# Attention with two kinds of heads, then a maxout network: another order for the first half batch and for each later step

## Chip, cores and metric

The kernel runs on one core of one Trainium2 chip. The metric is the device time of one execution in microseconds (us); before the change the median of three runs is 235.67 us (235.42 to 236.05).

## What is computed

Four batches of eight heads of causal attention over 768 positions with 64 numbers per head. Heads 0, 2 and 6 see every earlier position, the others only the first 4 positions and a window of the last 64. Each row of the result (8 heads x 64 = 512 numbers) then goes through a network that takes the largest of three products and multiplies that by a fourth matrix.

```python
scores = scale * np.matmul(q, k.transpose(0, 1, 3, 2))
stream_keep = causal & (is_sink | in_win)
mask = np.where(retr[0, :, 0, 0, None, None], full_mask, stream_mask)
scores = np.where(mask[None, :, :, :], scores, -1000000000.0)
...
return np.matmul(a, v).astype(np.float32)

h = np.maximum(np.maximum(x @ w1, x @ w2), x @ w3)
return (h @ w_out).astype(np.float32)
```

Here `x` is the attention's result as 3072 rows of 512, `w1` to `w3` are 512 x 768 and `w_out` is 768 x 512.

## The kernel before

**Steps.** The work is cut into 32 attention steps, numbered s. A step is one pair of heads in one half of one batch's rows (384 rows, three blocks of 128): steps 0 to 3 are the four head pairs of the first half of batch 0, steps 4 to 7 those of its second half, steps 8 to 11 the first half of batch 1, and so on. In a first half a step has two units of scores (0 and 1), in a second half, where a row also looks back at the first half, four (0 to 3). The score tiles `st` have two buffers in PSUM, so a unit of scores can only start when the exponential of the unit two before it has read its buffer. Transposes (`tr`), attention sums (`oacc`) and the network's results (`yy`) share four other PSUM buffers in turn.

**Stages of a step.** `load(s)` (L113) issues the DMAs of q and k for one pair of heads (192 KB each), and, once for each half batch, three DMAs of 256 KB for v of all eight heads. `prep(s)` (L283) casts k to fp16 on DVE (`kn`) and q on ACT (`qn`). `turn(s)` (L310) transposes both on PE, six matmuls, and copies the result to `KQ` on DVE. `scores(s, units)` (L329) does the score matmuls on PE, takes their exponential on ACT (into `pt`), and multiplies the blocks that need it by a 0/1 mask `mk`: on POOL, but for unit 1 of steps 0 to 3, which DVE does. `prep_v(s)` (L291) casts v (`va`; on ACT in steps 0 to 3, later on DVE) and makes on POOL a copy `vf` whose far blocks are zero for the windowed heads. `av(s)` (L380) multiplies `pt` by `va` or `vf` on PE; its seventh matmul is the first that reads `vf`. DVE then takes a reciprocal (`rc`) and a product (`x`). `turn_x(s)` (L407) transposes `x` on PE, and DVE copies it to `xT`.

**The network.** When the fourth head pair of a half batch is turned, `ffn` (L219) for its 384 rows is put into a queue of 24 units. A unit of the first 18 is four matmuls into one `yy` tile (L238) and its evacuation: ACT copies the product with the first matrix (L246), DVE takes the maximum with the other two (L249). The last six are three groups of six matmuls with `w_out` (L256), each followed by an ACT copy and an output DMA, and by an empty unit. For the first half batch the 18 units go matrix by matrix, so that the first six need only `w1`. `share(s, part, 3)` (L427) hands out these units at three places of each step, from step 5 on, 24 for each four steps.

**What sets the order.** Nothing reorders the program: each engine does its instructions in the order in which the loop at L447 writes them, and waits where an operand isn't ready. A step writes: the load for step s+7, `scores(s)` of units 0 and 1, `turn_x(s-2)`, a share, `turn(s+1)`, `av(s-1)`, a share, `prep(s+2)`, `scores(s)` of units 2 and 3, `prep_v(s+1)`, a share. In steps 1 to 4 `turn_x(s-1)` follows right behind `av(s-1)`. The masks of the head pairs 2 and 3 are built by `head_masks` (L195, four DVE instructions) in steps 1 and 2, and each of steps 0 to 3 ends with `load_weight` (L205), a DMA issued by POOL of one weight matrix (768 KB in fp16). All other loads and the outputs are issued by SP, but for q of steps 0 to 3 (ACT).

Of the kernel before, what the change touches and what calls it, by code (L numbers as in the profile page):

```python
# [10 lines left out]
FP32 = mybir.dt.float32  # L11
AF = mybir.ActivationFunctionType
ALU = mybir.AluOpType
# [35 lines left out]
def kernel(  # L49
# [32 lines left out]
    AHEAD = 7  # L82

    consts = ctx.enter_context(tc.tile_pool(name="consts", bufs=1))
    stage = ctx.enter_context(tc.tile_pool(name="stage", bufs=AHEAD + 1))
# [23 lines left out]

# [3 lines left out]
    def load(s):  # L113
        b, half, hp = where(s)
        hs, ts = slice(2 * hp, 2 * hp + 2), slice(half * HALF, (half + 1) * HALF)
        t = []
        for nm, src in (("ks", k), ("qs", q)):
            st = stage.tile([P, 2, HB, D], FP32, tag=nm, name=nm)
            eng = nc.scalar if s < NHP and nm == "qs" else nc.sync
            eng.dma_start(  # L120
                out=st, in_=src[b, hs, ts].rearrange("h (p j) d -> p h j d", p=P)
            )
            t.append(st)
        staged[s] = t
        if hp == 1:
            vs = stage.tile([P, H, HB, D], FP32, tag="vs", name="vs", bufs=3)
            for j in range(HB):
                r0 = half * HALF + j * P
                nc.sync.dma_start(
                    out=vs[:, :, j], in_=v[b, :, r0 : r0 + P].rearrange("h p d -> p h d")  # L130
                )
            staged_v[b, half] = vs
# [150 lines left out]
    def prep(s):  # L283
# [3 lines left out]
        nc.vector.tensor_copy(out=kn, in_=ks_.rearrange("p h j d -> p j h d"))  # L287
# [41 lines left out]
    def scores(s, us):  # L329
# [21 lines left out]
        for u, st in zip(us, sts):  # L351
# [4 lines left out]
            for at, u0, nu, cols, n, m0 in MASKED[half]:  # L356
                if at != u:
                    continue
                for hl_all in (slice(0, 2),):
                    if nu == 1 and len(cols) == 1:  # L360
                        x = pt[:, u0, hl_all, cols[0] : cols[0] + n]
                        m = mk[:, 2 * hp : 2 * hp + 2, m0 : m0 + n]
                    elif nu == 2:
                        x = pt[:, u0 : u0 + 2, :, cols[0] : cols[0] + n]
                        m = (
                            mk[:, 2 * hp : 2 * hp + 2, m0 : m0 + n]
                            .unsqueeze(1).to_broadcast([P, 2, 2, n])
                        )
                    else:
                        x = pt[:, u0].rearrange("p h (c n) -> p h c n", n=n)[:, :, 0:4:3]  # L370
                        m = (
                            mk[:, 2 * hp : 2 * hp + 2, m0 : m0 + n]
                            .unsqueeze(2).to_broadcast([P, 2, 2, n])
                        )
                    eng = nc.vector if s < NHP and u == 1 else nc.gpsimd
                    eng.tensor_tensor(out=x, in0=x, in1=m, op=ALU.mult)  # L376
# [30 lines left out]
    def turn_x(s):  # L407
        b, half, hp = where(s)
# [17 lines left out]

    def share(s, part, parts):  # L427
        if s < FIRST or s > NSTEP:
            return
# [16 lines left out]
    prep_v(0)  # L446
    for s in range(NSTEP + 2):  # L447
# [6 lines left out]
        if s > FIRST:  # L454
            turn_x(s - 2)
        share(s, 0, 3)
        if s + 1 < NSTEP:
            turn(s + 1)
        if 0 < s <= NSTEP:
            av(s - 1)  # L460
        if 0 < s < FIRST:
            turn_x(s - 1)
        share(s, 1, 3)
        if s + 2 < NSTEP:
            prep(s + 2)
        if live and n_u > 2:
            scores(s, [2, 3])
        if s + 1 < NSTEP:
            prep_v(s + 1)
        if 0 < s < NHP - 1:  # L470
            head_masks(s + 1)
        share(s, 2, 3)
        if s < 4:
            load_weight(s)
# [37 lines left out]
```

## Time and profile before

| | before |
|---|---|
| median of three runs | 235.67 us |
| the profiled execution | 235.46 us |
| its span, first to last instruction | 233.7 us |
| PE busy | 203.3 us (87%) |
| DVE, ACT, POOL busy | 144.2, 131.2, 121.0 us |

The profiled execution is 1.76 us longer than its span, which lies around the instructions. The profile has a page (busy time of each engine, the span in 40 slices, the chain of work that ended last, the costliest groups of instructions by line) and the trace answers for any stretch: busy time by window, what each engine waited for, and the instructions in order of time. A row of the order of time reads: start, duration, engine, line, operation, output<-inputs, form, count, and in square brackets how long the engine had been idle and on whom it waited. Neighbouring instructions of one kind are merged into one row. An engine name with q behind it (POOLq, SPq) or a DMA row is an issue, not the transfer.

### The profile page before, as it was taken

Reading aid. Unit: us, or ns where it says so; the run is one execution under the profiler, and the core shown is the slowest. Engines: PE = TensorE matmul, PEld = TensorE weight load, DVE = VectorE, ACT = ScalarE, POOL = GpSimd, SP = SyncE. Lnnn points to the kernel's source line nnn. Section 1 sums busy time; section 2 is a strip of 40 time slices with the busy share of each in tenths; the row PEclk is TensorE's granted clock in tenths of the full one; section 3 lists DMA queues with packets and bytes.
Section 4 is the critical chain, followed back from the end, with each engine's and each line's share of the span. In section 5 each row is a group of like instructions: output and inputs, shape, how many; then the busy total and the mean of one; then the engine's idle time right before and its main releaser. Section 6 shows DMA issues by size and latency. Waiting matters only on the chain.

```text
span 233.7 us, 5102 instructions
## 1 busy us (share of the span) xinstructions
PE 203.3 (87%) x2000; PEld 120.8 (52%) x2000; DVE 144.2 (62%) x306; ACT 131.2 (56%) x206; POOL 121.0 (52%) x137
## 2 busy tenths in 40 slices
PE   1335458999999999999999999999999999999993
PEld 0123333566556645655566545665566556555651
DVE  2437771488778854657689817766689636552540
ACT  3065347664675556785664586556655568742222
POOL 3066657256775717754777444577766276550000
PEclk9999999999999999999999999999999999999998
DMA  5999999980369226900497039402300120003003
GB/s 127 272 271 230 245 235 216 319 181 6 107 195 228 81 78 174 222 3 4 157 270 181 3 135 237 104 0 66 139 3 1 48 90 3 0 0 137 1 0 135
DMA packets 48359, 28.64 MB, mean 123 GB/s; under 512 B 26576, under 2 KB 45264, under 8 KB 48336
## 3 DMA queue, kind: packets, MB, share of 16 engines
q1 hardware_dynamic: 44736, 24.39, 39.3%
q0 software_dynamic: 2368, 3.15, 7.6%
q10 hardware_dynamic: 1232, 0.79, 1.2%
q8 instruction: 15, 0.25, 0.5%
q14 instruction: 8, 0.07, 0.1%
HBM read 25.17 MB, written 6.29 MB: 135 GB/s over the span
## 4 chain that ended last, share of the span: by engine, by line
PE 68%; ACT 11%; POOL 3%; issue 3%; DVE 2%; POOLq 0%; ACTq 0%; DVEq 0%
PE yy L238 34%; ACT pt L353 9%; PE oacc L391 8%; PE yy L256 8%; PE st L343 6%; PE tr L315 4%; POOL pt L376 3%; PE tr L416 3%; PE yst L238 3%; ACT qn L288 1%; PE yst L256 1%; DVE KQ L322 1%; DVE x L401 0%; POOLq L507 0%; DVE pt L376 0%
## 5 line engine op out<-in xcount | busy, mean ns | idle before, releaser
L376 POOL TENSOR_TENSOR pt<-pt,mk 128x512 f16<-128x512 f16 (+1 forms) x92 | 97.3, 1078 | 64.4 <-ACT pt L353 64.2
L353 ACT ACTIVATE pt<-st 128x1024 f16<-128x1024 f32 x96 | 82.5, 922 | 20.0 <-PE st L343 13.4
L246 ACT CAST acc<-yy 128x384 f16<-128x384 f32 x45 | 21.8, 488 | 44.4 <-PE yy L238 39.6
L343 PE MATMUL st<-KQ 64*128 64x384 f16 (+2 forms) x320 | 31.2, 297 | 11.3 <-DVE KQ L322 7.3
L238 PE MATMUL yy<-xT,w0t 128*128 128x384 f16 x180 | 38.1, 335 | 0.0
L249 DVE TENSOR_TENSOR acc<-yy,acc 128x384 f16<-128x384 f32 x45 | 24.8, 554 | 20.4 <-ACT acc L246 11.8
L322 DVE COPY KQ<-tr 128x768 f16<-128x768 f16 x32 | 30.4, 951 | 10.6 <-PE tr L315 10.6
L238 PE MATMUL yy<-xT,w1t 128*128 128x384 f16 x180 | 36.2, 326 | 0.0
L238 PE MATMUL yy<-xT,w2t 128*128 128x384 f16 x180 | 36.1, 326 | 0.0
L302 POOL TENSOR_TENSOR vf<-va,far 128x130 f16<-128x130 f16 (+1 forms) x32 | 20.0, 625 | 23.9 <-DVE va L300 14.2
L256 PE MATMUL yy<-woutt,hT 128*128 128x512 f16 x132 | 31.0, 379 | 0.0
L419 DVE COPY xT<-tr 128x384 f16<-128x384 f16 x32 | 11.4, 356 | 30.4 <-PE tr L416 30.4
L343 PEld LDWEIGHTS <-KQ 64*128 64x128 f16 x320 | 13.1, 98 | 32.5 <-issue 20.3
L391 PE MATMUL oacc<-va,pt 128*128 128x65 f16 x352 | 27.1, 199 | 0.8 <-POOL pt L376 0.4
L249 DVE TENSOR_TENSOR hT<-yy,acc 128x384 f16<-128x384 f32 x45 | 25.0, 555 | 3.3 <-PE yy L238 0.3
L391 PEld LDWEIGHTS <-pt 128*128 128x128 f16 x672 | 25.5, 100 | 1.6 <-POOL pt L376 1.2
L263 ACT COPY ot<-yy 128x512 f32<-128x512 f32 x22 | 12.9, 588 | 19.5 <-PE yy L256 19.5
L238 PEld LDWEIGHTS <-w0t 128*128 128x128 f16 x192 | 18.0, 100 | 10.9 <-issue 1.6
L238 PEld LDWEIGHTS <-w2t 128*128 128x128 f16 x192 | 17.8, 98 | 11.2 <-issue 0.8
L238 PEld LDWEIGHTS <-w1t 128*128 128x128 f16 x192 | 17.3, 97 | 11.8 <-issue 2.4
L391 PE MATMUL oacc<-vf,pt 128*128 128x65 f16 x320 | 22.1, 194 | 0.0
L256 PEld LDWEIGHTS <-hT 128*128 128x128 f16 x144 | 13.3, 98 | 14.6 <-issue 0.6
(46 smaller groups left out, 159.8 us busy)
## 6 DMA issues: line engine op xcount, KB each, us to landing
ks<-in_k_dram SPq DMA_DIRECT2D x32, 192.0 KB, 4.1
vs<-in_v_dram SPq DMA_DIRECT2D x24, 256.0 KB, 5.8
out_dram<-ot SPq DMA_DIRECT2D x24, 256.0 KB, 2.0
qs<-in_q_dram SPq DMA_DIRECT2D x28, 192.0 KB, 4.0
qs<-in_q_dram ACTq DMA_DIRECT2D x4, 192.0 KB, 6.2
w0t<-in_moe_w_dram POOLq DMA_DIRECT2D x1, 768.0 KB, 8.5
w1t<-in_moe_w_dram POOLq DMA_DIRECT2D x1, 768.0 KB, 10.0
w2t<-in_moe_w_dram POOLq DMA_DIRECT2D x1, 768.0 KB, 11.0
```

Source lines behind the costliest of these rows:

```text
L238: nc.tensor.matmul(yy[:, 0:HALF], w_t[wi][:, ks, ni * P : (ni + 1) * P], xT[b, half][ks], start=(ks == 0), stop=(ks == KS - 1),)
L246: nc.scalar.copy(out=acc[ni], in_=yy[:, 0:HALF])
L249: nc.vector.tensor_tensor(out=dst, in0=yy[:, 0:HALF], in1=acc[ni], op=ALU.max)
L256: nc.tensor.matmul(yo[:, 0:DMdl], hT[ns][:, tb * P : (tb + 1) * P], woutt[:, ns, :], start=(ns == 0), stop=(ns == NNB - 1),)
L263: nc.scalar.copy(out=ot, in_=yo[:, 0:DMdl])
L302: nc.gpsimd.tensor_tensor(out=vf[j][:, hs, k0:k1, 0 : D + 1], in0=va[j][:, hs, k0:k1, 0 : D + 1], in1=far[:, hs, k0:k1].unsqueeze(3).to_br ...
L322: nc.vector.tensor_copy(out=KQs[s].rearrange("p (i t j) -> p i t j", i=2, j=HB), in_=tr[:, 0:S].rearrange("p (i j t) -> p i t j", i=2, j=HB),)
L343: nc.tensor.matmul(st[:, hl, c0 : c0 + n * P], KT[ki // HB if half else 0][hb : hb + D, ki % HB * P : (ki % HB + 1) * P], KQ[hb : hb + D, ...
L353: nc.scalar.activation(out=pt[:, u, :, 0:w], in_=st[:, :, 0:w], func=AF.Exp, scale=sc)
L376: eng.tensor_tensor(out=x, in0=x, in1=m, op=ALU.mult)
L391: nc.tensor.matmul(o[:, qi, hl, 0 : D + 1], pt[:, u, hl, c : c + P], vv[:, 2 * hp + hl, ki, 0 : D + 1], start=(idx == 0), stop=(idx == len ...
L419: nc.vector.tensor_copy(out=xT[b, half][hp], in_=tr[:, 0:HALF])
```

## The change

It does five things.

1. **Loads.** q and k come for two pairs of heads at once (384 KB) from step 2 on, into tiles for four heads, six buffers of each; loads are issued eight steps ahead instead of seven; v is loaded behind q and k of the steps 2 and 3 in the first half batch, and at the first head pair of each later half batch.
2. **The first four steps** have a loop of their own. In it the masks are no longer part of `scores`: those on DVE stand behind `turn(s+1)` and `av(s-1)`. `turn_x` comes two steps late there too. `prep_v` of steps 0 and 1 stands behind the scores of step 1. `kn` of the steps 2, 3 and 4 is cast on ACT. The four mask-building instructions for the head pairs 2 and 3 stand together at the end of step 1.
3. **The weights** are issued in steps 1, 2, 4 and 4 instead of 0, 1, 2 and 3.
4. **The first network** starts in step 4 instead of step 5, because `turn_x` of steps 2 and 3 both stand there; a table `EARLY` hands out its 24 units as 7, 6, 4, 3 and 4 in steps 4 to 8.
5. **All later steps** write: `scores` of units 0 and 1, `turn_x(s-2)`, a share, `av(s-1)`, `scores` of units 2 and 3, `turn(s+1)`, a share, `prep_v(s)`, `prep(s+2)`, a share. So `av` comes before `turn`, the second two units of scores come right behind `av`, and `prep_v` is that of the same step, not of the next. (In steps 5 to 7 the second share stands ahead of `turn`, and in step 4 ahead of the second two units.)

How this moves rows on the engines:

ACT at the start, before: the casts of q for the steps 0 and 1, the cast of v (va), and only then the exponentials of step 0 (pt_192).

```order
L288 CAST qn_161<-qs_95 128x384
L288 CAST qn_180<-qs_101 128x384
L298 CAST va0_147<-vs_103 128x2x3x64
L353 ACTIVATE pt_192<-st_193 128x1024
L353 ACTIVATE pt_192<-st_198 128x2x256
L288 CAST qn_215<-qs_109 128x384
```

The same place now:

```order
L297 CAST qn_153<-qs_95 128x384
L297 CAST qn_172<-qs_101 128x384
L362 ACTIVATE pt_186<-st_187 128x1024
L362 ACTIVATE pt_186<-st_192 128x2x256
L294 CAST kn_209<-ks_103 128x384
L297 CAST qn_208<-qs_105 128x384
L362 ACTIVATE pt_213<-st_214 128x1024
L362 ACTIVATE pt_213<-st_219 128x2x256
L307 CAST va0_139<-vs_107 128x2x3x64 x2
```

The first cast of v has moved behind the exponentials of steps 0 (pt_186) and 1 (pt_213), and a cast of k has come in.

DVE in steps 0 to 2, before. pt<-pt,mk is a mask multiplication, KQ<-tr the copy of a turned q and k, x the product behind the reciprocal, xT the copy of a turned x:

```order
L376 TENSOR_TENSOR pt_192<-pt_192,mk_156 128x2x256
L322 COPY KQ_213<-tr_206 128x768
L287 CAST kn_216<-ks_107 128x384
L376 TENSOR_TENSOR pt_226<-pt_226,mk_156 128x2x256
L322 COPY KQ_247<-tr_240 128x768
L399 RECIPROCAL rc_262<-oacc_249 128x6
L401 TENSOR_TENSOR x_264<-oacc_249,rc_262 128x384
L419 COPY xT0_266<-tr_270 128x384
L287 CAST kn_276<-ks_111 128x384
L197 TENSOR_SCALAR mk_156<-kept_137,least_154 128x512 x2
```

The same place now:

```order
L331 COPY KQ_206<-tr_199 128x768
L383 TENSOR_TENSOR pt_186<-pt_186,mk_148 128x2x256
L331 COPY KQ_233<-tr_226 128x768
L406 RECIPROCAL rc_256<-oacc_243 128x6
L408 TENSOR_TENSOR x_258<-oacc_243,rc_256 128x384
L383 TENSOR_TENSOR pt_213<-pt_213,mk_148 128x2x256
L203 TENSOR_SCALAR mk_148<-kept_129,least_146 128x512 x4
L331 COPY KQ_292<-tr_285 128x768
L428 COPY xT0_294<-tr_298 128x384
```

Each KQ copy now stands ahead of the mask of the step before it; the casts of k are gone from here, and the four mask-building instructions stand together.

ACT in a later step of a second half, before (st_1345 and st_1350 are the units 0 and 1, st_1443 and st_1448 the units 2 and 3 of one step):

```order
L353 ACTIVATE pt_1344<-st_1345 128x1024
L353 ACTIVATE pt_1344<-st_1350 128x1024
L246 CAST acc_1374<-yy_1369 128x384
L246 CAST acc_1437<-yy_1432 128x384
L288 CAST qn_1439<-qs_859 128x384
L353 ACTIVATE pt_1344<-st_1443 128x1024
L353 ACTIVATE pt_1344<-st_1448 128x2x384
```

The same place now (units st_1311, st_1316, then st_1383 and st_1388):

```order
L362 ACTIVATE pt_1310<-st_1311 128x1024
L362 ACTIVATE pt_1310<-st_1316 128x1024
L252 CAST acc_1340<-yy_1335 128x384
L362 ACTIVATE pt_1310<-st_1383 128x1024
L362 ACTIVATE pt_1310<-st_1388 128x2x384
L252 CAST acc_1415<-yy_1410 128x384
```

One network copy and the cast of q no longer stand between the two pairs of exponentials.

```diff
--- before.py
+++ after.py
@@ -79,10 +79,10 @@
     assert (S, D, DMdl) == (768, 64, 512) and window <= P and n_sink <= P
     AT = [_where(0), _where(1)]
     NSTEP = B * 2 * NHP
-    AHEAD = 7
+    AHEAD = 8

     consts = ctx.enter_context(tc.tile_pool(name="consts", bufs=1))
-    stage = ctx.enter_context(tc.tile_pool(name="stage", bufs=AHEAD + 1))
+    stage = ctx.enter_context(tc.tile_pool(name="stage", bufs=6))
     half16 = ctx.enter_context(tc.tile_pool(name="half16", bufs=2))
     qkt = ctx.enter_context(tc.tile_pool(name="qkt", bufs=2))
     ptp = ctx.enter_context(tc.tile_pool(name="ptp", bufs=3))
@@ -106,26 +106,32 @@

     staged = {}
     staged_v = {}

     def load(s):
         b, half, hp = where(s)
-        hs, ts = slice(2 * hp, 2 * hp + 2), slice(half * HALF, (half + 1) * HALF)
+        t0 = half * HALF
+        n = 1 if s < 2 else 2
+        if s > 2 and hp % 2:
+            return
         t = []
         for nm, src in (("ks", k), ("qs", q)):
-            st = stage.tile([P, 2, HB, D], FP32, tag=nm, name=nm)
+            st = stage.tile([P, 4, HB, D], FP32, tag=nm, name=nm)
             eng = nc.scalar if s < NHP and nm == "qs" else nc.sync
             eng.dma_start(
-                out=st, in_=src[b, hs, ts].rearrange("h (p j) d -> p h j d", p=P)
+                out=st[:, 0 : 2 * n],
+                in_=src[b, 2 * hp : 2 * hp + 2 * n, t0 : t0 + HALF].rearrange(
+                    "h (p j) d -> p h j d", p=P
+                ),
             )
             t.append(st)
-        staged[s] = t
-        if hp == 1:
+        for i in range(n):
+            staged[s + i] = [x[:, 2 * i : 2 * i + 2] for x in t]
+        if hp == (0 if s >= NHP else 2):
             vs = stage.tile([P, H, HB, D], FP32, tag="vs", name="vs", bufs=3)
             for j in range(HB):
-                r0 = half * HALF + j * P
+                r0 = t0 + j * P
                 nc.sync.dma_start(
                     out=vs[:, :, j], in_=v[b, :, r0 : r0 + P].rearrange("h p d -> p h d")
                 )
@@ -284,7 +290,10 @@
         ks_, qs = staged.pop(s)
         qn = half16.tile([P, HB, 2, D], FP16, tag="qn", name="qn")
         kn = half16.tile([P, HB, 2, D], FP16, tag="kn", name="kn")
-        nc.vector.tensor_copy(out=kn, in_=ks_.rearrange("p h j d -> p j h d"))
+        if 2 <= s <= NHP:
+            nc.scalar.copy(out=kn, in_=ks_.rearrange("p h j d -> p j h d"))
+        else:
+            nc.vector.tensor_copy(out=kn, in_=ks_.rearrange("p h j d -> p j h d"))
         nc.scalar.copy(out=qn, in_=qs.rearrange("p h j d -> p j h d"))
         cast[s] = (kn, qn)

@@ -353,27 +362,25 @@
             nc.scalar.activation(
                 out=pt[:, u, :, 0:w], in_=st[:, :, 0:w], func=AF.Exp, scale=sc
             )
-            for at, u0, nu, cols, n, m0 in MASKED[half]:
-                if at != u:
-                    continue
-                for hl_all in (slice(0, 2),):
-                    if nu == 1 and len(cols) == 1:
-                        x = pt[:, u0, hl_all, cols[0] : cols[0] + n]
-                        m = mk[:, 2 * hp : 2 * hp + 2, m0 : m0 + n]
-                    elif nu == 2:
-                        x = pt[:, u0 : u0 + 2, :, cols[0] : cols[0] + n]
-                        m = (
-                            mk[:, 2 * hp : 2 * hp + 2, m0 : m0 + n]
-                            .unsqueeze(1).to_broadcast([P, 2, 2, n])
-                        )
-                    else:
-                        x = pt[:, u0].rearrange("p h (c n) -> p h c n", n=n)[:, :, 0:4:3]
-                        m = (
-                            mk[:, 2 * hp : 2 * hp + 2, m0 : m0 + n]
-                            .unsqueeze(2).to_broadcast([P, 2, 2, n])
-                        )
-                    eng = nc.vector if s < NHP and u == 1 else nc.gpsimd
-                    eng.tensor_tensor(out=x, in0=x, in1=m, op=ALU.mult)
+            if s >= NHP:
+                masks(s, u)
+    def masks(s, us, eng=None):
+        b, half, hp = where(s)
+        pt = pts[s]
+        for at, u0, nu, cols, n, m0 in MASKED[half]:
+            if at != us:
+                continue
+            m = mk[:, 2 * hp : 2 * hp + 2, m0 : m0 + n]
+            if nu == 1 and len(cols) == 1:
+                x = pt[:, u0, :, cols[0] : cols[0] + n]
+            elif nu == 2:
+                x = pt[:, u0 : u0 + 2, :, cols[0] : cols[0] + n]
+                m = m.unsqueeze(1).to_broadcast([P, 2, 2, n])
+            else:
+                x = pt[:, u0].rearrange("p h (c n) -> p h c n", n=n)[:, :, 0:4:3]
+                m = m.unsqueeze(2).to_broadcast([P, 2, 2, n])
+            (eng or nc.gpsimd).tensor_tensor(out=x, in0=x, in1=m, op=ALU.mult)

     xs = {}

@@ -405,6 +412,8 @@
         xs[s] = x

     def turn_x(s):
+        if s not in xs:
+            return
         b, half, hp = where(s)
         if hp == 0:
             xT[b, half] = [
@@ -424,8 +433,14 @@

     FIRST = NHP + 1

+    EARLY = [(0, 3, 4), (2, 2, 2), (1, 1, 2), (1, 1, 1), (1, 1, 2)]
     def share(s, part, parts):
-        if s < FIRST or s > NSTEP:
+        if s < FIRST + NHP:
+            fill(EARLY[s - NHP][part])
+            return
+        if s > NSTEP:
             return
         s0 = s - (s - FIRST) % NHP
         ws = [(5, 7, 6)[where(i)[1] if i < NSTEP else 2] for i in range(s0, s0 + NHP)]
@@ -443,35 +458,59 @@
     head_masks(0)
     prep(1)
     head_masks(1)
-    prep_v(0)
-    for s in range(NSTEP + 2):
+    for s in range(NHP):
+        load(s + AHEAD)
+        if s > 1:
+            prep_v(s)
+        scores(s, [0, 1])
+        masks(s, 0)
+        turn(s + 1)
+        if s > 1:
+            turn_x(s - 2)
+        if s == 1:
+            prep_v(0)
+            prep_v(1)
+        prep(s + 2)
+        if s > 0:
+            av(s - 1)
+        masks(s, 1, nc.vector)
+        if s == 1:
+            head_masks(2)
+            head_masks(3)
+        if 0 < s < 3:
+            load_weight(s - 1)
+    for s in range(NHP, NSTEP + 2):
         live = s < NSTEP
         if s + AHEAD < NSTEP:
             load(s + AHEAD)
         if live:
             n_u = len(UNITS[where(s)[1]])
             scores(s, [0, 1])
-        if s > FIRST:
-            turn_x(s - 2)
+        turn_x(s - 2)
         share(s, 0, 3)
+        if s <= NSTEP:
+            av(s - 1)
+        if s == NHP:
+            turn_x(s - 1)
+            load_weight(2)
+            share(s, 1, 3)
+        if live and n_u > 2:
+            scores(s, [2, 3])
+        early = s < 2 * NHP
+        if NHP < s and early:
+            share(s, 1, 3)
         if s + 1 < NSTEP:
             turn(s + 1)
-        if 0 < s <= NSTEP:
-            av(s - 1)
-        if 0 < s < FIRST:
-            turn_x(s - 1)
-        share(s, 1, 3)
+        if not early:
+            share(s, 1, 3)
+        if live:
+            prep_v(s)
         if s + 2 < NSTEP:
             prep(s + 2)
-        if live and n_u > 2:
-            scores(s, [2, 3])
-        if s + 1 < NSTEP:
-            prep_v(s + 1)
-        if 0 < s < NHP - 1:
-            head_masks(s + 1)
         share(s, 2, 3)
-        if s < 4:
-            load_weight(s)
+        if s == NHP:
+            load_weight(3)
     while queue:
         fill(1)
```

## The prediction

> **What bounds the kernel now.** I read the slices of the page first, then the windows, then what PE waited for, then the rows of one early step in order of time.
>
> ```profile
> PE   1335458999999999999999999999999999999993
> ...
> 0.00:38.30 38.30, 15.79 (x143) 9.60 (x144) 20.72 (x49) 16.31 (x26) 17.54 (x29) 1.00 1.07 230
> 38.30:62.90 24.60, 24.17 (x274) 14.91 (x273) 15.09 (x31) 16.11 (x24) 14.59 (x15) 1.00 0.64 152
> 62.90:85.50 22.60, 22.60 (x207) 13.26 (x204) 19.03 (x40) 12.37 (x21) 14.14 (x17) 1.00 0.54 147
> 85.50:112.80 27.30, 26.12 (x296) 15.81 (x296) 15.53 (x32) 19.36 (x29) 15.86 (x16) 1.00 0.42 112
> ...
> 212.00:233.75 21.75, 17.78 (x102) 9.65 (x100) 7.19 (x14) 5.80 (x11) 0.00 (x0) 0.96 0.16 62
> ```
>
> A window row gives its length, then the busy time of PE, PEld, DVE, ACT and POOL. PE is idle 30.4 us of 233.7 (the table above), and 22.5 of these (38.30 - 15.79) lie ahead of 38.3 us, where the network starts. In the steps of a second half (85.5 to 112.8) it loses 1.2 us, in those of a first half (62.9 to 85.5) none, and at the end 4.0 us, which the change does not touch. So time can come from the start, and about 3 us from the second halves. What PE waited for, up to 38.3 us and then in the window from 85.5:
>
> ```profile
> PE tr L416 <- DVE x L401: 8.4, 4, 2.6
> PE st L343 <- DVE KQ L322: 7.3, 2, 6.2
> PE tr L315 <- DVE kn L287: 5.5, 4, 4.6
> ...
> PE st L343 <- ACT pt L353: 0.9, 3, 0.3
> ```
>
> Three long waits at the start all end with a DVE row. One early step shows the round that they make:
>
> ```profile
> 15.55 0.82 PE L343 MATMUL st<-KQ 64*128 64x384 f16 x6 [6.22 <-DVE KQ L322]
> 16.20 1.51 ACT L353 ACTIVATE pt<-st 128x1024 f16<-128x1024 f32 x2 [1.78 <-PE st L343]
> 17.32 1.96 POOL L376 TENSOR_TENSOR pt<-pt,mk 128x512 f16<-128x512 f16 x2 [0.91 <-ACT pt L353]
> 17.75 1.00 DVE L376 TENSOR_TENSOR pt<-pt,mk 128x512 f16<-128x512 f16 x1 [1.79 <-ACT pt L353]
> 18.67 0.94 DVE L322 COPY KQ<-tr 128x768 f16<-128x768 f16 x1
> 19.54 0.18 DVE L399 RECIPROCAL rc<-oacc 128x6 f32<-128x6 f32 x1
> 19.75 0.56 DVE L401 TENSOR_TENSOR x<-oacc,rc 128x384 f16<-128x384 f32 x1
> 20.36 0.50 PE L416 MATMUL tr<-ident,x 128*128 128x128 f16 x3 [2.58 <-DVE x L401]
> 20.80 0.82 PE L343 MATMUL st<-KQ 64*128 64x384 f16 x6
> 20.90 0.36 DVE L419 COPY xT<-tr 128x384 f16<-128x384 f16 x1 [0.59 <-PE tr L416]
> ```
>
> Scores, exponential, mask, KQ copy, rc and x, turn_x, next scores: 5.25 us a step (15.55 to 20.80), in which no engine is full. The copy waits behind the mask on DVE, and the next scores behind turn_x on PE.
>
> **The start, laid out again.** Up to 9.3 us nothing moves: scores(0) are done by 7.84, q of step 1 is cast by 8.43, the first masks are built, turn(1) ends at 9.33.
>
> ```profile
> 7.02 0.82 PE L343 MATMUL st<-KQ 64*128 64x384 f16 x6 [1.05 <-DVE KQ L322]
> 7.92 0.51 ACT L288 CAST qn<-qs 128x384 f16<-128x384 f32 x1 [2.51 <-DMA qs<-in_q_dram]
> 8.37 0.61 DVE L197 TENSOR_SCALAR mk<-kept,least 128x512 f16<-128x512 f16 x2
> 8.80 0.53 PE L315 MATMUL tr<-ident,qn 128*128 128x128 f16 x3
> 11.69 0.51 ACT L298 CAST va<-vs 128x384 f16<-128x384 f32 x1 [3.26 <-DMA vs<-in_v_dram]
> 12.11 1.50 ACT L353 ACTIVATE pt<-st 128x1024 f16<-128x1024 f32 x2
> 19.23 0.40 POOL L302 TENSOR_TENSOR vf<-va,far 128x130 f16<-128x130 f16 x1
> ```
>
> *Step 0.* ACT stood 3.26 us before v; its exponentials now follow the cast at 8.43 and end at 9.94. KQ(1), ahead of the mask, is copied 9.35 to 10.30, and scores(1) start at 10.35 instead of 15.55.
>
> *Step 1.* ACT casts kn and qn (2 x 0.51, to 10.96), then exp(1) 11.0 to 12.5. turn(2) ends at 12.0, KQ(2) at 12.95. **A new wait:** on PE av(0) now stands ahead of scores(2), and its seventh matmul needs vf(0), which POOL makes behind the masks of step 1: POOL starts on the first unit at about 12.1 (1.1 behind the exponentials' start, as 17.32 behind 16.20), 1.96 of masks bring it to 14.05, 0.40 of vf to 14.45. The rest of av(0) ends near 15.0, and scores(2) start there instead of at 20.80. Queued behind that wait are turn(3) and turn_x(0). v itself now comes behind 384 KB of k, so I let it land at 13.0 instead of 11.6, so that its cast ends at 13.5, still ahead of 14.05.
>
> *Steps 2 to 4.* DVE sets the pace: rc and x 0.77, mask, four mask-building rows (2 x 0.61, once), KQ 0.94, xT 0.36. The mask row is the unsure one. Taken alone:
>
> ```profile
> 17.32 1.14 POOL L376 TENSOR_TENSOR pt<-pt,mk 128x512 f16<-128x512 f16 x1 [0.91 <-ACT pt L353]
> ...
> 27.86 1.14 POOL L376 TENSOR_TENSOR pt<-pt,mk 128x512 f16<-128x512 f16 x1 [2.23 <-ACT pt L353]
> ...
> 28.34 0.94 DVE L376 TENSOR_TENSOR pt<-pt,mk 128x512 f16<-128x512 f16 x1 [0.86 <-ACT pt L353]
> ```
>
> POOL's first row ends at 18.46 and 29.00, DVE's mask at 18.75 and 29.28: both times 0.28 to 0.29 later, whether it began at 17.75 or 28.34. So the mask costs between 0.28 (POOL quiet) and 1.0 (as now). With 1.0, scores(3) and scores(4) start at 18.97 and 22.1, x(3) is ready at 26.45, and after turn_x(3) the first network matmul starts at 27.0; with 0.28 at 25.3. The delayed masks fall where POOL runs vf or issues a weight, so I lean to the short end: **26.3**, instead of 38.29.
>
> This fits "Who interferes with whom" in SBUF — State Buffer of the Trainium skill: a DVE instruction with two SBUF inputs and a POOL instruction that reads SBUF take one port in turn, and the second waits for the whole first. By that rule in full the start would be 25.3 and the total 222.9; by the row's full length 27.0 and 224.6. The trace agrees in the two pairs above.
>
> **What is not yet done at that point.** At 38.29 the kernel before had finished work that now comes later:
>
> ```profile
> 35.32 0.93 PE L343 MATMUL st<-KQ 64*128 64x384 f16 x6
> 37.04 1.31 PE L343 MATMUL st<-KQ 64*128 64x384 f16 x8 [0.80 <-ACT pt L353]
> 38.29 2.74 PE L238 MATMUL yy<-xT,w0t 128*128 128x384 f16 x8
> 42.18 1.46 PE L238 MATMUL yy<-xT,w0t 128*128 128x384 f16 x8
> ```
>
> Scores 4 (units 2, 3), scores 5 and turn(5) (two rows such as the one of 0.53 above, overlapping: 0.8): 3.0 us at the early rate. The first eight network matmuls took 2.74 us and the same eight later 1.46, so this work, now behind them, should take some 1.8; and one more network unit may run at the slow rate (0.7). Of 12.0 us, 38.29 - 26.3, there remain 12.0 - 2.5 = **9.5 us**.
>
> **Transfers under it.** By the layout POOL issues w0t behind vf(0) and vf(1) at 14.9, w1t behind the masks of step 2 at 19.3, w2t behind the first mask of step 4 at 25.6, and woutt near 35.
>
> ```profile
> w0t<-in_moe_w_dram POOLq DMA_DIRECT2D x1, 768.0 KB, 8.5
> w1t<-in_moe_w_dram POOLq DMA_DIRECT2D x1, 768.0 KB, 10.0
> w2t<-in_moe_w_dram POOLq DMA_DIRECT2D x1, 768.0 KB, 11.0
> ...
> ks<-in_k_dram SPq DMA_DIRECT2D x1, 192.0 KB, 15.6
> ```
>
> The last number is the time to landing: 23.4, 29.3 and 36.6. The first six units use w0t, from 26.3; w1t is wanted at about 33, w2t at about 39 (12 units of 0.73, and the attention work of steps 4 and 5). Cover: 3, 4 and 2.5 us; every us beyond costs itself. The paired q and k loads save issues on SP, which waits for nothing that is late: nothing.
>
> **Steps 5 to 8.** They get 6, 4, 3 and 4 units instead of about 6, so a step can be as short as 5 us, against POOL's three masks of 1.14 and its vf, 4.3 in all, and av must find vf of the step before. I take 0.4 us of new waits (0 to 1).
>
> ```profile
> 89.93 0.85 POOL L302 TENSOR_TENSOR vf<-va,far 128x390 f16<-128x390 f16 x1
> ...
> L353 ACT ACTIVATE pt<-st 128x1024 f16<-128x1024 f32 x96 | 82.5, 922 | 20.0 <-PE st L343 13.4
> ```
>
> **Later steps.** Before, the units 2 and 3 came late in a step, and the next scores waited 0.3 us for their exponentials, three times in each second half. Now they come right behind av: between the two pairs of scores PE has turn_x, a share (two units, 1.46) and the thirty matmuls of av, over 2 us, against two exponentials (2 x 0.92, the mean in the second row), and turn and two shares on the other side. Idle in the four second halves is 0.4 us (38.3 to 62.9) and about 1.2, three times. The wait for ACT is 0.9 of each of the three and all of the 0.4, 3.1 us; I take **2.5 us** of it (0 to 3.1, or a loss, see the rivals). In first halves PE has no idle time to gain; what is moved there is turn behind av, and its KQ copy behind rc and x. It must be done when the next scores start, about 1.4 us later: by an estimate from the early rows at half their length (scores 0.4, turn_x 0.3, av 0.4) and two units (1.46) av ends 2.5 us into a step, rc, x and KQ (1.7) at 4.2, and the step lasts 22.6 / 4 = 5.65. That is its cover.
>
> **Sum.** 235.46 (profiled; 0.21 below the median shown, 1.76 above its span) - 9.5 - 2.5 + 0.4 = **223.9 us**.
>
> **Rivals.**
> - *The one port, the other way.* At 17 us the four mask-building rows on DVE meet POOL's masks of step 2. They never met before. If each side waits for a whole row, KQ(3) is 1.15 us later: 223.9 + 1.2 = 225.1. For it: the two pairs above. Against: they read one SBUF tile, where the mask reads two. By the same section of the Trainium skill such an instruction can take the port too, in its two-port modes; no run here shows it.
> - *Transfers.* Loads beside a weight were slow before (15.6 us for a k load issued at 18.75, in the last row above). If the larger loads now hold back w2t by 5 to 6 us in turn, PE waits 3: 227. For it: DMA engines are busy throughout (1.07). Against: same bytes, same order of the weights.
> - *Later order gains nothing*, because av now brings its wait for POOL ahead of the second scores: 223.9 + 2.5 = 226.4.
> - *Slower.* DVE is busy 19.03 of 22.60 in first halves. If the KQ copy, now behind rc and x, comes later than its 1.4 us of cover in each of these 12 later steps, PE waits there. A wait of 1 us per step, that is a KQ 2.4 us later than laid out, eats the whole gain: 223.9 + 12 = 235.9. It decides from 1.4 us on. Against: DVE has the same instructions there in nearly the same order, and PE had no wait.
> - *The start does not shorten* beyond step 0 (3.3 us and one of the steps), because av(0)'s wait for vf repeats: 230. Against: from step 2 on, vf stands ahead of the masks.
>
> **Chances.** Forecast (222.4 to 225) 52%, port 13%, transfers 15%, later order without gain 14%, start not shortened 3%, slower 3%. The low end: mask 0.28 (-1.0), all 3.1 us (-0.6), no new waits (-0.4), no cost for the slow rate (-0.7) is 221.2, so 221; the upper end takes in the transfers with some more: 228.5. A measurement here can tell 0.3% (0.7 us) from nothing. Faster by more 96%, within 1%, slower 3%.
>
> **What would show it.** First network matmul near 26.3 us; scores of steps 1 and 2 near 10.4 and 15; short DVE masks; no wait of PE for a weight; no waits of scores for ACT in second halves, PE full in first halves. I am wrong if PE waits for a weight row, or if scores wait for KQ in the steps from 8 on.

## The result, and the profile after

| | before | changed |
|---|---|---|
| median of four runs | 235.86 us (235.42 to 236.17) | 222.14 us (221.67 to 222.99) |
| ratio, with its 95% interval | | 0.9424 (0.939 to 0.9457) |
| the profiled execution | 235.46 us | 222.99 us |
| its span | 233.7 us | 221.3 us |

The kernel became 5.8% faster; 223.9 us was predicted, with 221 to 228.5 as the range. The median lies 0.3 us below the narrower band, 222.4 to 225, to which the prediction gave 52%. Two of the experiments' profiled executions (changed_again and early_other) ran at a granted clock of 0.78 and 0.59 instead of 0.997; nothing is read from their traces, and their times are left out.

The slices of PE and the windows of the changed kernel, cut at the places that answer to those of before (length, then the busy time of PE, PEld, DVE, ACT, POOL):

```profile
PE   1366799988999999999999999989999999999991
...
0.00:26.10 26.10, 12.76 (x123) 8.52 (x124) 16.46 (x41) 14.88 (x25) 13.29 (x24) 1.00 1.03 227
26.10:51.30 25.20, 23.58 (x248) 13.99 (x246) 17.08 (x32) 17.29 (x25) 16.36 (x17) 1.00 1.13 238
51.30:73.80 22.50, 22.37 (x240) 13.87 (x240) 18.20 (x40) 13.44 (x23) 14.93 (x19) 1.00 0.86 231
73.80:99.70 25.90, 25.33 (x262) 15.19 (x260) 17.73 (x34) 18.41 (x27) 16.50 (x16) 1.00 0.25 73
```

The stretch ahead of the network has gone from 38.3 to 26.1 us, and PE's idle time in it from 22.5 to 13.3. The next stretch is 0.6 longer (25.2 for 24.6). A second half (73.8 to 99.7) is shorter by 1.4, though not cut at quite the same matmul. What PE waited for, up to 27 us and then from 26 to 198 us:

```profile
PE tr L324 <- DVE kn L296: 5.3, 2, 4.7
PE st L352 <- DVE KQ L331: 3.9, 3, 1.8
PE oacc L398 <- ACT va L307: 1.6, 1, 1.6
PE tr L425 <- DVE x L408: 1.3, 2, 0.9
...
PE yy L262 <- DVE hT L255: 1.9, 2, 1.0
PE st L352 <- DVE KQ L331: 1.1, 1, 1.1
PE tr L425 <- DVE x L408: 0.9, 1, 0.9
PE oacc L398 <- DVE hT L255: 0.6, 1, 0.6
```

The wait of turn_x for x fell from 8.4 to 1.3 us, that of scores for KQ from 7.3 to 3.9. (The 0.9 us of turn_x in the second list is the longest wait of the first once more; the two windows share one us.) From 26 us on there is no wait of scores for an exponential any more and none for a weight, but there are new ones, all for DVE: 1.9 us for hT (the last maximum of the network, which the matmuls with `w_out` read), 1.1 for a KQ, 0.6 for a buffer. The round of an early step, beside that of before:

```profile
15.30 0.82 PE L352 MATMUL st<-KQ 64*128 64x384 f16 x6
15.64 0.56 DVE L408 TENSOR_TENSOR x<-oacc,rc 128x384 f16<-128x384 f32 x1
15.95 1.51 ACT L362 ACTIVATE pt<-st 128x1024 f16<-128x1024 f32 x2 [0.28 <-PE st L352]
16.09 0.42 POOL L311 TENSOR_TENSOR vf<-va,far 128x130 f16<-128x130 f16 x1
16.11 0.69 DVE L383 TENSOR_TENSOR pt<-pt,mk 128x512 f16<-128x512 f16 x1
16.67 0.53 PE L425 MATMUL tr<-ident,x 128*128 128x128 f16 x3
16.72 2.05 DVE L203 TENSOR_SCALAR mk<-kept,least 128x512 f16<-128x512 f16 x4
17.47 1.83 POOL L383 TENSOR_TENSOR pt<-pt,mk 128x512 f16<-128x512 f16 x2 [0.96 <-ACT pt L362]
18.69 0.94 DVE L331 COPY KQ<-tr 128x768 f16<-128x768 f16 x1
19.70 0.82 PE L352 MATMUL st<-KQ 64*128 64x384 f16 x6 [1.84 <-DVE KQ L331]
```

The scores of this step no longer stand behind x: turn_x comes after them, and finds x ready. What sets this step is DVE's row of four mask-building instructions, 2.05 us instead of twice 0.61, because it runs into POOL's masks at 17.47; the KQ copy stands behind it.

To see where the time went, two places are followed through both traces at which PE has the same work behind it in either order: the first scores of step 9, when the whole first network is done, and the reciprocal behind av of step 31, the last. First before, then changed:

```profile
65.45 0.50 PE L343 MATMUL st<-KQ 64*128 64x384 f16 x6
211.35 0.20 DVE L399 RECIPROCAL rc<-oacc 128x6 f32<-128x6 f32 x1 [2.07 <-PE oacc L391]
...
56.07 0.50 PE L352 MATMUL st<-KQ 64*128 64x384 f16 x6
198.17 0.20 DVE L406 RECIPROCAL rc<-oacc 128x6 f32<-128x6 f32 x1 [1.57 <-PE oacc L398]
```

9.38 us are gained by step 9 and 13.18 by step 31, so 3.80 on the way. (The reciprocal of step 8 would not do as the first place: before, the turn of step 10 and its KQ copy stand ahead of it, now behind it.) The profiled execution shows only 12.47 of it, because its last output took 0.8 us longer to land (2.0 us before, 2.8 now, from issue to landing).

235.46 - 13.18 = 222.28, which is within 0.2 of the median of the runs.

### The profile page after: what moved, and what is told of

Read it like the earlier page. It is cut to its first block, busy times and chain, and to the rows that moved or that the text cites. A ratio compares the mean times of both kernels' runs of the same rounds, so it can differ in the third digit from the quotient of the medians.

```text
span 221.3 us, 5034 instructions
## 1 busy us (share of the span) xinstructions
PE 199.5 (90%) x2000; PEld 120.9 (55%) x2000; DVE 146.7 (66%) x303; ACT 134.2 (61%) x209; POOL 122.6 (55%) x137
## 4 chain that ended last, share of the span: by engine, by line
PE 81%; DVE 7%; DMA 3%; ACT 3%; issue 2%; POOL 1%; ACTq 0%
PE yy L244 38%; PE yy L262 12%; PE st L352 10%; PE oacc L398 9%; PE tr L324 4%; PE tr L425 4%; DMA qs<-in_q_dram 3%; PE yst L244 3%; DVE KQ L331 2%; ACT pt L362 2%; PE yst L262 1%; DVE kn L296 1%; DVE hT L255 1%; DVE mk L203 1%; DVE x L408 1%
## 5 line engine op out<-in xcount | busy, mean ns | idle before, releaser
L383 POOL TENSOR_TENSOR pt<-pt,mk 128x512 f16<-128x512 f16 (+1 forms) x92 | 98.3, 1088 | 64.5 <-ACT pt L362 64.4
L352 PE MATMUL st<-KQ 64*128 64x384 f16 (+2 forms) x320 | 28.4, 291 | 5.2 <-DVE KQ L331 5.0
L398 PEld LDWEIGHTS <-pt 128*128 128x128 f16 x672 | 26.4, 100 | 7.0 <-issue 3.5
L398 PE MATMUL oacc<-va,pt 128*128 128x65 f16 x352 | 26.5, 199 | 1.6 <-ACT va L307 1.6
L244 PEld LDWEIGHTS <-w1t 128*128 128x128 f16 x192 | 18.0, 98 | 11.4 <-issue 1.2
L262 PEld LDWEIGHTS <-hT 128*128 128x128 f16 x144 | 13.6, 98 | 17.2 <-DVE hT L255 2.9
L352 PEld LDWEIGHTS <-KQ 64*128 64x128 f16 x320 | 11.4, 97 | 19.9 <-DVE KQ L331 7.4
```

The source lines that it names most:

```text
L244: nc.tensor.matmul(yy[:, 0:HALF], w_t[wi][:, ks, ni * P : (ni + 1) * P], xT[b, half][ks], start=(ks == 0), stop=(ks == KS - 1),)
L262: nc.tensor.matmul(yo[:, 0:DMdl], hT[ns][:, tb * P : (tb + 1) * P], woutt[:, ns, :], start=(ns == 0), stop=(ns == NNB - 1),)
L352: nc.tensor.matmul(st[:, hl, c0 : c0 + n * P], KT[ki // HB if half else 0][hb : hb + D, ki % HB * P : (ki % HB + 1) * P], KQ[hb : hb + D, ...
L383: (eng or nc.gpsimd).tensor_tensor(out=x, in0=x, in1=m, op=ALU.mult)
L398: nc.tensor.matmul(o[:, qi, hl, 0 : D + 1], pt[:, u, hl, c : c + P], vv[:, 2 * hp + hl, ki, 0 : D + 1], start=(idx == 0), stop=(idx == len ...
```

## The experiments

Each is the changed kernel with one edit, unless it says otherwise. A ratio is to the kernel before in the same set; that of the changed kernel is 0.9424, and 0.9419 (0.9386 to 0.9453) in its second timing.

**The v cast first.** The theory: each of three edits at the start carries a part. The first to be undone is ACT's order.

```diff
-        if s > 1:
+        if s != 1:
             prep_v(s)
         scores(s, [0, 1])
...
-            prep_v(0)
             prep_v(1)
```

> The changed kernel, but the first cast of v stands ahead of the exponentials of step 0 on ACT again, as before. Theory: these exponentials wait for v (near 13.0 instead of 9.2 us), scores of step 2 come near 17.2 instead of 15.3, total 224 to 225. Rival (av of step 0 waits for v and vf in any case, so nothing was gained there): 222.1.

Measured: 226.97 us (226.15 to 227.8), ratio 0.9602 (0.9564 to 0.964). The rival falls. The order of time of ACT, and one row of DVE further on:

```profile
13.34 0.51 ACT L307 CAST va<-vs 128x384 f16<-128x384 f32 x1 [4.19 <-DMA vs<-in_v_dram]
13.76 1.02 ACT L362 ACTIVATE pt<-st 128x1024 f16<-128x1024 f32 x1
...
20.30 2.31 DVE L203 TENSOR_SCALAR mk<-kept,least 128x512 f16<-128x512 f16 x1
```

ACT stands 4.19 us before v, as it stood 3.26 before the change. The scores of step 2 come at 17.68 instead of 15.30, near the 17.2 expected, and the first network matmul at 30.59 instead of 26.08. That is 4.5 us, more than expected, and the time is above the 224 to 225 expected: behind the late start the four mask-building rows on DVE meet more of POOL's rows. One of them, 0.34 us in quiet, lasts 2.31, and KQ of step 3 waits behind it.

**The mask ahead of the copy.**

```diff
         masks(s, 0)
+        masks(s, 1, nc.vector)
         turn(s + 1)
...
             av(s - 1)
-        masks(s, 1, nc.vector)
```

> The changed kernel, but in steps 0 to 3 the mask on DVE stands ahead of the KQ copy again, as before; turn_x stays two steps late. Theory (DVE order is one of the two causes of the early round): KQ of step 4 waits until POOL's first mask row of step 3 and then DVE's mask are done, 1.6 us later than now, that of step 2 1.5 us later but under the wait for vf: total 223.7 to 224.6. Rival (only turn_x held the round): 222.1.

Measured: 227.62 us (226.81 to 228.25), ratio 0.9636 (0.9605 to 0.9667). The rival falls, and the size that I expected was too small. The pair of DVE rows of step 0:

```profile
10.88 0.99 DVE L383 TENSOR_TENSOR pt<-pt,mk 128x512 f16<-128x512 f16 x1 [1.31 <-ACT pt L362]
11.80 0.95 DVE L331 COPY KQ<-tr 128x768 f16<-128x768 f16 x1
```

The mask now lies beside POOL's and is long in every step, 0.88 to 0.99 us. In three of the four steps DVE stands 1.3 to 2.3 us for the exponential, and then the KQ copy stands behind the mask; in the other it is busy with the mask-building rows instead. I had counted two steps, not four. The first network matmul is at 30.09, 4.0 us later.

**turn_x one step late.**

```diff
-        if s > 1:
-            turn_x(s - 2)
...
             av(s - 1)
+            turn_x(s - 1)
         masks(s, 1, nc.vector)
```

> The changed kernel, but in steps 0 to 3 turn_x comes one step late, right behind av, as before; the DVE order of the masks stays. Theory (PE standing at turn_x until rc and x are done is the other cause of the early round): scores of steps 2, 3 and 4 each wait about 1 to 1.4 us more, the first network matmul comes near 29, total 224.5 to 226. Rival (only the mask ahead of the copy held the round): 222.1.

Measured: 225.32 us (224.86 to 225.68), ratio 0.9539 (0.952 to 0.9559), the first network matmul at 28.15. What PE waited for up to 28.4 us, two lines:

```profile
PE tr L425 <- DVE x L408: 4.5, 4, 1.5
PE st L352 <- DVE KQ L331: 2.1, 2, 1.1
```

The time is as expected, and the rival falls: turn_x waits 4.5 us for x in four rows instead of 1.3 in two. The first network matmul is 0.85 us earlier than the 29 expected, and a wait of the changed kernel is shorter under the new one: scores wait 2.1 us for KQ instead of 3.9.

**The later steps in the order of before.** The loop's body of before, for s from 8 on:

```diff
+        if s >= 2 * NHP:
...
+            turn_x(s - 2)
+            share(s, 0, 3)
+            if s + 1 < NSTEP:
+                turn(s + 1)
+            if s <= NSTEP:
+                av(s - 1)
+            share(s, 1, 3)
...
+                prep(s + 2)
...
+                scores(s, [2, 3])
...
+                prep_v(s + 1)
+            share(s, 2, 3)
+            continue
```

> The changed kernel, but the steps from 8 on written in the order of before (turn ahead of av, the second two units of scores and the next step's prep_v late). Theory (the later order gives about 0.95 us in each of the last three second halves, by the starts of the reciprocals in the two traces): 222.1 + 2.9 = 225.0 us (224.5 to 225.5), PE waiting for exponentials 0.3 us three times in each second half again, the first network matmul unchanged near 26.1. Rival (the whole gain is made in the first eight steps and merely carried on): 222.1.

Measured: 224.83 us (224.59 to 227.07), ratio 0.9541 (0.9493 to 0.9588): 2.7 us more than the changed kernel, near the 2.9 expected. What PE waited for from 60 to 197 us:

```profile
PE st L352 <- ACT pt L362: 2.5, 8, 0.3
```

The waits for exponentials are back, eight of 0.3 us, and those for hT are gone. A wait costs more than it shows. Eight score matmuls of step 15 that are interrupted by one (before), and uninterrupted (changed):

```profile
102.10 0.40 PE L343 MATMUL st<-KQ 64*128 64x384 f16 x4
102.80 0.39 PE L343 MATMUL st<-KQ 64*128 64x384 f16 x4 [0.31 <-ACT pt L353]
...
91.40 0.61 PE L352 MATMUL st<-KQ 64*128 64x384 f16 x8
```

They take 1.09 us instead of 0.61, so 0.48 is lost where the list of waits has 0.31. From the scores of step 9 to the reciprocal of step 31 the trace of this run falls 3.70 us behind the changed one (from 0.24 to 3.94), more than the medians differ; it is the trace of its slowest run.

**The loads of before**, with the old `load`, seven steps ahead, eight buffers.

> The changed kernel with the loads of before: q and k for one pair of heads at a time, seven steps ahead, v at the second head pair. Theory (the loads carry nothing of the gain; av of step 0 is held by vf, not by a load): 221.3 to 222.4 us, q of step 1 cast near 8.0 to 8.4 instead of 8.8, w0t still landing before the first network matmul. Rival (the paired loads are a part of the gain): above 223.

Measured: 223.6 us (221.88 to 224.66), ratio 0.9461 (0.9406 to 0.9515), too wide to tell. So it was run again.

> The changed kernel with the loads of before, a second time with more rounds, since the first (a median of 223.6, 221.9 to 224.7) could not tell. Theory (the loads carry nothing): within 0.7 us of the changed kernel of this set. Rival (paired loads are worth something): 1 to 2 us above it.

Measured: 222.09 us (221.98 to 224.09), ratio 0.9419 (0.939 to 0.9449), the same ratio as the changed kernel of that set. The cast of q of step 1 began at 8.02 us in the first of the two traces, as expected, and not at 8.81. But k of step 2 came late there. This is ACT's row in loads_again:

```profile
12.30 0.51 ACT L287 CAST kn<-ks 128x384 f16<-128x384 f32 x1 [2.37 <-DMA ks<-in_k_dram]
```

The exponentials of step 1 stand behind it on ACT, and the turn waited for it 1.9 and 1.7 us in the two traces. The first network matmul came at 27.32 and 27.12, 1.0 to 1.2 later than 26.08. The time does not show it, because the first twelve network matmuls took 2.23 us in both and 3.49 in the changed kernel (more on this at the end). So the paired loads carry nothing that these runs can measure in the time, though the theory that no load holds this start is not what the traces show.

**The mask-building rows apart.** This asks whether DVE and POOL hold each other up, and what it costs.

```diff
         if s == 1:
             head_masks(2)
+        if s == 2:
             head_masks(3)
```

> The changed kernel, but the two mask-building rows for the last head pair stand at the end of step 2, not all four at the end of step 1. Theory (DVE and POOL wait for each other's whole rows, which made the fourth of these rows 1.26 us long instead of 0.34): KQ of step 3 is copied near 17.4 instead of 18.7, the first network matmul comes 0.5 to 1.3 us earlier, total 220.9 to 221.7. Rival (the long row costs nothing, something else ends later): 222.1.

```profile
16.44 0.60 DVE L203 TENSOR_SCALAR mk<-kept,least 128x512 f16<-128x512 f16 x2
16.97 0.94 DVE L331 COPY KQ<-tr 128x768 f16<-128x768 f16 x1
...
19.17 1.14 DVE L203 TENSOR_SCALAR mk<-kept,least 128x512 f16<-128x512 f16 x2
...
21.24 1.03 PE L352 MATMUL st<-KQ 64*128 64x384 f16 x8 [1.48 <-DVE KQ L331]
...
25.00 3.64 PE L244 MATMUL yy<-xT,w0t 128*128 128x384 f16 x12
```

The two rows left in step 1 are short again, and KQ of step 3 starts at 16.97 instead of 18.69. But the two that were moved to step 2 meet POOL there and take 1.14 us instead of 0.60, and now the scores of step 4 wait 1.48 us for KQ, where in the changed kernel those of step 3 waited 1.84. The first network matmul comes at 25.00, 1.08 earlier, and the reciprocal of step 31 is still 0.93 earlier; the traces of kernels with the same start lie nearly as far apart (25.64 to 26.65, see the end). The runs gave 222.55 us (221.84 to 223.42), ratio 0.9425 (0.9388 to 0.9462): no difference from the changed kernel, and the expected 220.9 to 221.7 was missed. That these rows hold each other up is shown by the trace; a gain in time is not.

**The cast of v at its old place, and on ACT in second halves.** In the changed kernel the waits for hT had this look (DVE, POOL and PE in step 15):

```profile
97.75 1.16 POOL L383 TENSOR_TENSOR pt<-pt,mk 128x512 f16<-128x512 f16 x1
98.14 0.98 DVE L309 CAST va<-vs 128x384 f16<-128x384 f32 x1
99.04 0.54 DVE L296 CAST kn<-ks 128x384 f16<-128x384 f32 x1
99.51 0.54 DVE L255 TENSOR_TENSOR hT<-yy,acc 128x384 f16<-128x384 f32 x1
100.10 0.39 PE L262 MATMUL yy<-woutt,hT 128*128 128x512 f16 x1 [0.98 <-DVE hT L255]
```

The cast of v begins in the middle of one of POOL's masks, lasts 0.98 us instead of 0.35, and pushes the last maximum, for which PE then stands 0.98 us. Two edits go at it. The first moves `prep_v`, so with the cast also POOL's vf; the second changes nothing but the engine of the cast.

```diff
-        if live:
+        if s == NHP:
             prep_v(s)
         if s + 2 < NSTEP:
             prep(s + 2)
+        if s + 1 < NSTEP:
+            prep_v(s + 1)
```

> The changed kernel, but from step 4 on the cast of v is that of the next step again, behind the casts of k and q, as before. Theory (where the cast of v stands now, in second halves, it runs beside POOL's masks and takes 0.53 to 1.33 us instead of 0.35, which holds the maxima behind it on DVE and through them PE): casts of 0.35 again, no waits of PE for hT, total 220.3 to 221.6. Rival (the place of this cast is free): 222.1; or slower, where vf then comes late.

```diff
-        if s < NHP:
+        if s < NHP or half:
             nc.scalar.copy(out=vdst, in_=vs[:, hs])
```

> The changed kernel, but ACT casts v in second halves, not DVE. Theory (the long casts come from DVE and POOL sharing a way to SBUF that ACT doesn't use): the cast takes 0.51 us there beside POOL's masks, and the waits of PE for hT go: 220.3 to 221.6. Rival (any engine's cast slows beside the masks, or ACT, 18.4 of 25.9 us busy there, has no room for four more casts): 222.1 or more.

Measured: 220.22 us (219.02 to 221.4), ratio 0.9324 (0.9278 to 0.937) at the old place, and 218.16 us (217.94 to 220.58), ratio 0.9236 (0.9208 to 0.9263) on ACT. The forms of the cast, for the first on DVE from 74 to 200 us, for the second on ACT and then on DVE (shortest, median and longest in ns):

```profile
L309 DVE CAST va<-vs x18: 349/533/1185, 81.9 to 185.0; 128x384 f16<-128x384 f32 x18
...
L307 ACT CAST va<-vs x20: 507/515/536, 14.0 to 193.2; 128x384 f16<-128x384 f32 x20
L309 DVE CAST va<-vs x12: 349/350/370, 56.2 to 166.5; 128x384 f16<-128x384 f32 x12
```

At the old place the cast is not short again, so that expectation fails, though the time came out a little below it; it only pushes less that PE waits for (hT: 1.0 us in two waits instead of 1.9). On ACT no cast is longer than 0.54 us, though the masks run as before, and the waits for hT are gone. What PE waited for from 27 to 198 us with the cast on ACT:

```profile
PE st L352 <- DVE KQ L331: 1.1, 1, 1.1
PE oacc L398 <- POOL vf L311: 0.2, 1, 0.2
```

That settles the cause of these waits: a cast on DVE beside a mask on POOL. It doesn't settle the whole size. Between the reciprocals of steps 4 and 31 the two traces differ by 2.36 us (0.71 later to 1.65 earlier). The waits that are gone (1.9 for hT, 0.6 for the buffer, less the 0.2 that is new) account for that. The medians differ by 4.0. Both traces are of the slowest run of their kernel, 222.99 and 220.58 us, which differ by 2.4; the other four runs with the cast on ACT took 217.94 to 218.3 us, and what sets them apart is open.

**Another table for the first network.**

```diff
-    EARLY = [(0, 3, 4), (2, 2, 2), (1, 1, 2), (1, 1, 1), (1, 1, 2)]
+    EARLY = [(0, 3, 4), (2, 2, 2), (1, 1, 1), (1, 1, 1), (2, 2, 1)]
```

> The changed kernel with another table for the first network: steps 6, 7 and 8 get 3, 3 and 5 units, so that the third share of step 7 holds a group of six matmuls and not the empty unit. Theory (scores of step 8 wait 1.05 us for KQ because nothing stands between turn of that step and them): that wait goes, 0.6 to 1.1 us less than the changed kernel of this set. Rival (the step is bounded by POOL's masks and vf, so the wait only moves to av): no difference.

Measured: ratio 0.9393 (0.9364 to 0.9421), beside 0.9419 (0.9386 to 0.9453) for the changed kernel of the same set: the right sign, but not told from nothing.

> The changed kernel itself once more, as the measure for the other three of this set: 222.1 us (221.3 to 223.0).

That run gave 221.29 to 223.44 us with a median of 223.27, a little above the 221.3 to 223.0 expected; its ratio is 0.9419, as said.

**Three edits together**: the cast on ACT, the mask-building rows apart and this table.

> The changed kernel with three edits: ACT casts v in second halves, the mask-building rows of the last head pair stand in step 2, and the other table for the first network. Theory (the three waits stand at different places and add): 2.2 to 4 us for the cast, 0.9 for the masks, 0.6 to 1.1 for the table, together 216.2 to 218.4 us. Rival (they hide one another): about 218.2, that of the cast alone.

Measured: 219.14 us (218.06 to 219.64), ratio 0.9267 (0.9242 to 0.9291). That is no better than the cast on ACT alone, so the rival stands: what the other two edits gain can't be seen in the time. In its trace no wait of scores for KQ is left at step 8, but one of 0.53 us has come up a step earlier, where step 6 has one unit less. The fastest kernel found is the changed one with the cast on ACT, at 0.9236.

## Why the prediction was right, point by point

- **The start.** First network matmul predicted at 26.3, found at 26.08. Scores of step 1: 10.35 against 10.93 (q of step 1 landed later); of step 2: 15.0 against 15.30, held last by vf(0), as laid out. The cast of v was to end at 13.5 and only began at 13.51, so that PE first waited 1.56 us for it; POOL's masks, which end at 14.46, still set vf(0). That the three edits each carry a part is shown by undoing them: the first network matmul moves by 4.5 (ACT's order), 4.0 (DVE's) and 2.1 us (turn_x). The rows of v and vf in the changed kernel:

```profile
13.51 0.92 ACT L307 CAST va<-vs 128x384 f16<-128x384 f32 x2 [0.41 <-issue]
14.07 0.49 PE L398 MATMUL oacc<-va,pt 128*128 128x65 f16 x6 [1.56 <-ACT va L307]
14.88 0.21 PE L398 MATMUL oacc<-vf,pt 128*128 128x65 f16 x1 [0.32 <-POOL vf L311]
```

- **The DVE mask.** Taken between 0.28 and 1.0. Found: 0.97 in step 0, then 0.69, 0.41 and 0.41. So the shortest such row is 0.41, and 0.28 was too low. The three that count here are at the short end, as was argued, but the number did not follow the argument: 26.3 lies nearer to 27.0 (long masks) than to 25.3 (short ones).
- **The rival of the one port**, given 13%, came true as a mechanism beside the forecast: the fourth mask-building row met POOL's masks, and scores of step 3 began at 19.70, where 18.97 was laid out with long masks. The short masks made up for it. That the start came out within 0.3 us is therefore in part luck: one row too long, two shorter than the number assumed. The runs with these rows apart, and with the cast of v on ACT, agree with the rule of the Trainium skill that is cited there.
- **Work not yet done at that point**: mis-sized. It was charged with 1.8 us and another slow network unit with 0.7. The first twelve network matmuls took 3.49 us, where before the first eight took 2.74 and four more 0.73: no further slow unit, so this 0.7 was not due. Of the 12.21 us by which the first network matmul is earlier, 9.38 are left at step 9. That is 2.83 less, and the new waits of the next point are 1.7 of it, so that about 1.1 remain where 2.5 was charged; a gain of the new order in steps 5 to 7 may be hidden in this.
- **Transfers.** No wait of PE for a weight. Right: the cover held.
- **Steps 5 to 8**: 0.4 us forecast; 1.7 found (0.6 for a buffer, 1.1 for KQ of step 8). The step overlooked is that the third share of step 7 holds the empty unit, so that nothing stands between turn(8) and the scores that need it. With the other table, in the trace of the three edits together, that wait is gone. Up to step 9 the gain is 9.38 where 9.5 - 0.4 was forecast, but this agreement comes from two errors that cancel: too much charged for the work not yet done, too little for the new waits.
- **Later steps**: 2.5 forecast, from 0 to 3.1; 3.80 found between step 9 and step 31 by the traces, 2.7 by undoing the order and comparing medians. No wait for exponentials is left. This term was too small, in part because it took each wait at the 0.3 us that PE stood, where an interrupted group of scores loses 0.48; the rest was not followed. Not foreseen either is what this order gave back: 1.9 us of waits for hT. Two of the three second halves have such a wait and gain 0.95 and 1.05 us with it; the third has none and gains 1.80.
- **Slower rival**: its sign, a wait of scores for KQ from step 8 on, did come, once: 1.05 us at step 8, from the table and not from av and turn changing places, since the scores of the steps after 8 never waited for KQ. There its cover held.

The sum was 11.6 us; 13.2 by the same places in both traces. Of the 1.6 more, 1.3 lie in the later steps and 0.3 ahead of step 9. The mechanisms of the sum are the ones found; of its terms only the start came out in size by itself, and that in part by luck.

## What to carry to other kernels

Where an early stretch leaves every engine half idle, follow one round of it in order of time: each place where an in-order queue puts work that is wanted later ahead of work that the next round wants can be moved, and the layout by rows of the trace was right within 0.8 us at each step. After such a move ask what now runs at the same time: here the new order gave back time wherever a DVE row from SBUF to SBUF came to lie beside POOL's, 1.9 us of waits for hT alone. And compare two orders only at places where both have the same work behind them. An engine whose rows keep their length beside POOL's (here ACT's casts, 0.51 to 0.54 us) can take such a row at its plain price.

## What the runs showed of the hardware that was not expected

A DVE row can wait more than one POOL row long: 2.31 us for an instruction that takes 0.34 in quiet (v_cast_first, at 20.30, beside a vf of 0.42 and two masks that end at 22.45). In the changed kernel casts of v on DVE took 0.35 to 0.37 us in first halves and 0.47 to 1.33 in second halves, while the casts of k, of the same size but read in another order, kept to 0.54 to 0.55 throughout.

The same twelve first network matmuls took 3.49, 3.64 and 2.23 us in three of these kernels (changed, masks_built_apart, prep_v_next):

```profile
26.08 3.49 PE L244 MATMUL yy<-xT,w0t 128*128 128x384 f16 x12
...
25.64 2.23 PE L244 MATMUL yy<-xT,w0t 128*128 128x384 f16 x12
```

The second row is of prep_v_next, whose start is the same work in the same order. In both slow kernels the first of these matmuls followed each other every 0.32 us; late in the changed kernel four of this form take 0.65, 0.16 each. The granted clock in the profile does not separate them: over these matmuls it is 1.00 in the changed kernel and in prep_v_next, and 0.50 (up to 28 us) in masks_built_apart.

"What's actually happening" in TensorE: Matmul & The Clock Gate of the Trainium skill says that PE runs at half rate until it has been busy for a window that runs freely, not from the kernel's start. A difference of 1.3 us between equal starts agrees with that; no run here tests it.

The first network matmul itself comes at 25.64 to 26.65 us in the four traces that have the same order up to it (prep_v_next, changed, later_as_before at 26.30, v_cast_on_act at 26.65). So one profile cannot tell a difference of about 1 us at the start from nothing.
